# Attention and feed-forward on one core: four attention visits per tile, the first value copy on another queue, one mask tile

## The chip, the cores and the metric

The kernel runs on one core of one Trainium2 chip. The metric is device time in microseconds of one execution; lower is better. The kernel before took 334.62 us (median of 3 runs, 332.96 to 336.87). Its profiled execution has a span of 328.2 us, and all times inside the profile count from the start of that span.

The core has five engines that run side by side and wait for one another through semaphores. TensorE multiplies matrices (rows PE for matmuls and PEld for weight loads), VectorE (DVE) and ScalarE (ACT) work on elements, GpSimd (POOL) casts and copies here and issues transfers, and SyncE (SP) issues transfers. Matmul results go to PSUM banks; everything else lives in SBUF.

## What is computed

```python
# attention: batch 8, heads 8, sequence 576, head size 64; a query sees keys at most 32 away
scores = (1 / sqrt(64)) * q @ k.T
scores = where(abs(pos[:, None] - pos[None, :]) <= 32, scores, -1e9)
attn = exp(scores - max(scores));  attn = attn / (sum(attn) + 1e-9)
x = (attn @ v) laid out as (4608 tokens, 512)
# feed-forward: 512 -> 2048 -> 512
h = x @ w_in
g = 0.5 * h * (1 + tanh(sqrt(2/pi) * (h + 0.044715 * h**3)))
out = g @ w_out
```

## The kernel before

The 4608 tokens are nine FFN tiles of 512 (t = 0 to 8). While tile t is in its second FFN product, the attention of batch b = t + 1 is done in between. A plan says before which FFN-out matmul (0 to 111) which step comes: `s` scores and their exp, `m` mask, `v` weighted sum of values, `x` spread of the result into `xT`. The digit is the pair of heads (0 to 3); 4 is the batch's tail of queries for all pairs, and -1 is the tail of the batch before. A group of `s` and `v` at one place is called a visit below: TensorE leaves the FFN matmuls and comes back.

```python
PLAN = {5: "s0 v-1", 25: "m0 x-1", 27: "s1 v0", 40: "m1 x0", 49: "s2 v1", 62: "m2 x1",
        71: "s3 v2", 84: "m3 x2", 93: "s4 v3", 105: "m4", 112: "x3"}
PLAN_0 = {0: "w0 w1 m0", 10: "s-1 m-1", 16: "s1 v-1 w2 m1 x-1", 24: "s2 v0 w3 x0", 32: "m2 s3 v1 x1",
          40: "m3 v2 x2", 48: "t4", 51: "v3 c1 x3", 57: "s4 c2 m4"}      # tile 0

def score(b, g):
    m, prs, steps, slots, q0, n = work_of(b, g)
    ps = psS.tile([128, 2, 512], FP32, name="ps_s", tag=score_bank())    # S0 and S1 in turn
    ...                                                                  # 16 small matmuls: QT, KT -> ps
    nc.scalar.activation(pe, ps[:, :, 0:w], AF.Exp, scale=SCALE)

def mask(b, g, hs=slice(0, 2)):
    m, prs = work_of(b, g)[0:2]
    pe = groups[(b, g)][:, hs, :].rearrange("k h (r q) -> k (h r) q", r=len(prs))
    nc.vector.tensor_tensor(
        pe, pe, m.rearrange("k (o j) p -> k o (j p)", o=1).broadcast_to(list(pe.shape)), op=ALU.mult)

def weigh(b, g, other=False):
    ...
    o = bank(1) if other else psO.tile([128, 512], FP32, name="ps_o", tag="O")
    d = psO.tile([128, 512], FP32, name="ps_d", tag="D")
    ...                                   # d: 2 matmuls ones x pe; o: 14 (tail: 8) matmuls V x pe

def invert(b, g, o, d):                   # lt = exp(-ln(d)), two ScalarE instructions
def spread(b, g, o, lt):                  # xT = o * lt, on VectorE
```

There is one bank `O` and one bank `D`, and two pairs of score banks, `S0` and `S1`. The masks are four tiles, each built from pieces of a band `full`:

```python
kinds = [MAIN, TAIL, MAIN_0, TAIL_0]
masks = [const.tile([128, 4, n], FP16, name=f"mask{i}") for i, n in enumerate((120, 24, 128, 16))]
for i, q0 in ((2, 0), (3, 128), (0, 0), (1, 120)):
    for step in kinds[i]:
        for half, piece in enumerate(step):
            if piece is not None:
                ...
                nc.vector.tensor_copy(masks[i][r, :, p0 - q0:p1 - q0], full[r, :, pp0:pp0 + p1 - p0])
```

Queries and keys of batches 2 and on are loaded on SyncE's queue, cast by VectorE and transposed by transfers on SyncE's queue. Values are loaded, with a cast, on GpSimd's queue; then a copy inside SBUF puts each block also beside its neighbour on the other 64 partitions:

```python
def load_qk(b):                           # qr, four kr, qt, kt: seven transfers
    nc.sync.dma_start(...)
def load_v(b):                            # five transfers
    nc.gpsimd.dma_start(V[:, c, :, :], v[b, ...])
def pair_v(b, copy, hs=slice(0, H)):
    V = Vs[b % 2]
    copy(V[64:128, 4:8, hs, :], V[64:128, 0:4, hs, :])
    copy(V[0:64, 4:7, hs, :], V[0:64, 1:4, hs, :])

for t in range(NT):
    b = t + 1
    ...
        for fc in range(begun, NF):
            ffn_in(t, fc)
            if t == 1 and fc == 6:        # a gate: no load of batch 2's values before this gelu
                nc.gpsimd.tensor_copy(after, gTs[1][:, column(1, 5), 0:1])
                load_v(2)
                unpaired.append(2)
    if t and b + 1 < B:
        load_qk(b + 1)
    if t == 1:
        pair_v(unpaired.pop(), nc.sync.dma_start)
    ...                                   # the plan and the FFN-out matmuls; in v-1: load_v(b + 1)
    if unpaired:
        pair_v(unpaired.pop(), nc.sync.dma_start)
```

The first attention (batch 0) comes before any FFN work. It alternates transposes of the next pair (`turn`), their copies out (`trans_out`), masks, value pairing (`paired`) and `spin`, matmuls without use that keep TensorE busy:

```python
score(0, 0); spin(2, 512); pt = turn(1)
mask(0, 0)
trans_out(0, 1, pt)
spin(4, 512); score(0, 1); cast_vt(0); spin(2, 512); pt = turn(2)
paired(0)
mask(0, 1)
trans_out(0, 2, pt)
weighed(0); score(0, 2); spread(0, 0, *ods[0]); spin(5, 512)
paired(1); weighed(1); pt = turn(3)
trans_out(0, 3, pt)
mask(0, 2)
spin(3, 512, score=True); score(0, 3); spread(0, 1, *ods[1])
paired(2); weighed(2); mask(0, 3); ffn_in(0, 0, 0, 2); spread(0, 2, *ods[2])
paired(3); weighed(3)
```

Of the kernel before, what the change touches and what calls it, by code (L numbers as in the profile page):

```python
# [36 lines left out]
def cut(b):  # L37
# [5 lines left out]

PLAN = {5: "s0 v-1", 25: "m0 x-1", 27: "s1 v0", 40: "m1 x0", 49: "s2 v1", 62: "m2 x1",
        71: "s3 v2", 84: "m3 x2", 93: "s4 v3", 105: "m4", 112: "x3"}

TURN_0 = {10: 0, 12: 1, 14: 2, 15: 3}
PLAN_0 = {0: "w0 w1 m0", 10: "s-1 m-1", 16: "s1 v-1 w2 m1 x-1", 24: "s2 v0 w3 x0", 32: "m2 s3 v1 x1",
          40: "m3 v2 x2", 48: "t4", 51: "v3 c1 x3", 57: "s4 c2 m4"}

ORDER_0 = ([(t4, 4 * w + i) for w in range(4) for t4 in (0, 1)
            for i in ((2, 3, 0, 1) if w == 0 else range(4))] +
# [7 lines left out]
def kernel(  # L64
# [45 lines left out]
    full = const.tile([128, 4, 56], FP16, name="full")  # L110
    ones = const.tile([128, 64], FP16, name="ones")
    after = const.tile([128, 1], FP16, name="after")
    kinds = [MAIN, TAIL, MAIN_0, TAIL_0]
    masks = [const.tile([128, 4, n], FP16, name=f"mask{i}") for i, n in enumerate((120, 24, 128, 16))]
    KTs = [const.tile([128, NPAIR, 576], FP16, name=f"KT{i}") for i in range(2)]

    Vs = [const.tile([128, 8, H, 64], FP16, name=f"V{i}") for i in range(2)]
# [102 lines left out]
    def spin(n, width, score=False):  # L220
        ps = psS.tile([128, 2, 512], FP32, name="spin2", tag="S0")[:, 0, :] if score else \
            psO.tile([128, 512], FP32, name="spin", tag="O")
        for _ in range(n):
# [10 lines left out]
    nc.gpsimd.memset(idn, 0.0)  # L234
    nc.gpsimd.affine_select(out=idn, in_=idn, compare_op=ALU.not_equal, fill=1.0,
                            base=0, pattern=[[-1, 128]], channel_multiplier=1)
    for i, q0 in ((2, 0), (3, 128), (0, 0), (1, 120)):
        for step in kinds[i]:
            for half, piece in enumerate(step):
                if piece is not None:  # L240
                    k0, p0, p1 = piece
                    r, pp0 = slice(64 * half, 64 * half + 64), p0 - ((k0 - 64 * half) // 4 - 8)
                    nc.vector.tensor_copy(masks[i][r, :, p0 - q0:p1 - q0], full[r, :, pp0:pp0 + p1 - p0])  # L243
    nc.vector.memset(ones, 1.0)

    halfs = {}
# [50 lines left out]
    def bank(i):  # L297

        return psM.tile([128, 512], FP32, name="mm", tag=f"x{i}")
# [29 lines left out]


    groups = {}
    turns = [0]

    def score_bank():
        turns[0] ^= 1
        return f"S{turns[0] ^ 1}"


    def work_of(b, g):

        if g < 4:
            return (masks[0], [g], MAIN, SLOTS, 0, 120) if b else (masks[2], [g], MAIN_0, SLOTS_0, 0, 128)
        p0 = cut(b)
        return (masks[1 if b else 3], range(NPAIR), TAIL if b else TAIL_0, [(7, p0, 144)], p0, 144 - p0)

    def score(b, g):
        m, prs, steps, slots, q0, n = work_of(b, g)
        ps = psS.tile([128, 2, 512], FP32, name="ps_s", tag=score_bank())
        for r, pr in enumerate(prs):
            for step in steps:  # L350
                for half, piece in enumerate(step):
                    if piece is None:
                        continue
                    k0, p0, p1 = piece
                    for h in range(2):
                        r0 = 64 * h
                        nc.tensor.matmul(  # L357
                            ps[64 * half:64 * half + 64, h, 4 * n * r:4 * n * r + 4 * n].rearrange(
                                "k (j p) -> k j p", j=4)[:, :, p0 - q0:p1 - q0],
                            KTs[b % 2][r0:r0 + 64, pr, k0:k0 + 64],  # L360
                            QTs[b][r0:r0 + 64, pr, :, p0:p1], start=True, stop=True)
        w = 4 * n * len(prs)
        pe = ap_.tile([128, 2, w], FP16, name="pe", tag="pe") if g < 4 else \
            tailp.tile([128, 2, w], FP16, name="pet")
        nc.scalar.activation(pe, ps[:, :, 0:w], AF.Exp, scale=SCALE)  # L365
        groups[(b, g)] = pe

    def mask(b, g, hs=slice(0, 2)):
        m, prs = work_of(b, g)[0:2]
        pe = groups[(b, g)][:, hs, :].rearrange("k h (r q) -> k (h r) q", r=len(prs))  # L370
        nc.vector.tensor_tensor(  # L371
            pe, pe, m.rearrange("k (o j) p -> k o (j p)", o=1).broadcast_to(list(pe.shape)), op=ALU.mult)

    def weigh(b, g, other=False):
        m, prs, steps, slots, q0, n = work_of(b, g)
        pe = groups.pop((b, g))
        o = bank(1) if other else psO.tile([128, 512], FP32, name="ps_o", tag="O")
        d = psO.tile([128, 512], FP32, name="ps_d", tag="D")
        for h in range(2):
            nc.tensor.matmul(d[64 * h:64 * h + 64, 0:4 * n * len(prs)], ones, pe[:, h, :],  # L380
                             start=True, stop=True)
        for r, pr in enumerate(prs):
            cols = slice(4 * n * r, 4 * n * r + 4 * n)
            for i, (slot, p0, p1) in enumerate(slots):
                for h in range(2):
                    nc.tensor.matmul(  # L386
                        o[64 * h:64 * h + 64, cols].rearrange("d (j p) -> d j p", j=4)[:, :, p0 - q0:p1 - q0],
                        Vs[b % 2][:, slot, 2 * pr + h, :],
                        pe[:, h, cols].rearrange("k (j p) -> k j p", j=4)[:, :, p0 - q0:p1 - q0],
                        start=True, stop=True)  # L390
        return o, d
# [228 lines left out]
        pair_v(0, nc.vector.tensor_copy, slice(2 * g, 2 * g + 2))  # L620

    ods = {}
    score(0, 0)
    spin(2, 512)
    pt = turn(1)
    mask(0, 0)
    trans_out(0, 1, pt)
    spin(4, 512)
    score(0, 1)
    cast_vt(0)  # L630
    spin(2, 512)
    pt = turn(2)
    paired(0)
    mask(0, 1)
    trans_out(0, 2, pt)
    weighed(0)
    score(0, 2)
    spread(0, 0, *ods[0])
    spin(5, 512)
    paired(1)  # L640
    weighed(1)
    pt = turn(3)
    trans_out(0, 3, pt)
    mask(0, 2)
    spin(3, 512, score=True)
    score(0, 3)
    spread(0, 1, *ods[1])
    paired(2)
    weighed(2)
    mask(0, 3)  # L650
    ffn_in(0, 0, 0, 2)
    spread(0, 2, *ods[2])
    paired(3)
    weighed(3)
    for fc in (1, 2, 3):
        ffn_in(0, fc, 0, 2)
# [36 lines left out]
                       psO.tile([128, 8, 128], FP16, name="pt", tag="O"))  # L693
        ffn_in(0, fc)
    load_table(exp_set)
    score(1, 0)


    begun = 0
    for t in range(NT):  # L700
        b = t + 1
        att = b < B
        if t:
# [5 lines left out]
                cast_and_turn(b)  # L709
            for fc in range(begun, NF):  # L710
                ffn_in(t, fc)
                if t == 1 and fc == 6:

                    nc.gpsimd.tensor_copy(after, gTs[1][:, column(1, 5), 0:1])
                    load_v(2)
                    unpaired.append(2)
        plan = PLAN_0 if not t else PLAN if att else {5: "v-1", 31: "x-1"} if t == B - 1 else {}
# [6 lines left out]
        if t and b + 1 < B:  # L724
            load_qk(b + 1)
        if t == 1:
            pair_v(unpaired.pop(), nc.sync.dma_start)
        ods = {}
        for i in range(113 if t else 65):
            for act in plan.get(i, "").split():  # L730
                kind, g = act[0], int(act[1:])
                if kind == "w":
                    cast_w(wo[g], w_out16[:, 4 * g:4 * g + 4, :])
                    if g == 2:
# [7 lines left out]
                        cast_tails(1, nc.gpsimd)  # L742
                        load_qk(2)
                elif kind == "t":
                    pt = psS.tile([128, 2, 8, 128], FP16, name="pt", tag=score_bank())
                    trans_tails(1, pt[:, 0])
                elif kind == "c":
                    if g == 1:
                        combine_w()
                    combine(g)  # L750
                elif kind == "s":
                    score(*group(g))
                elif kind == "m":
                    mask(*group(g))
                elif kind == "v":
                    bb, gg = group(g)
                    o, d = weigh(bb, gg)
                    ods[g] = (o, invert(bb, gg, o, d))
                    if t and g < 0 and b + 1 < B:
                        load_v(b + 1)  # L760
# [49 lines left out]
```

The softmax here doesn't subtract the row's maximum and nothing guards it: scores larger than these inputs give would overflow.

## Time and profile before

| stretch of the span, us | what runs | length, us | TensorE busy, us | mean granted clock |
|---|---|---|---|---|
| 0 to 42 | first attention, FFN-in of tile 0 | 42.00 | 33.80 | 1.00 |
| 42 to 64.6 | FFN-out of tile 0 with batch 1 | 22.60 | 19.86 | 1.00 |
| 64.6 to 77.5 | FFN-in of tile 1 | 12.90 | 12.90 | 1.00 |
| 77.5 to 113.2 | FFN-out of tile 1 with batch 2 | 35.70 | 20.02 | 0.81 |
| 113.2 to 144.5 | tile 2 with batch 3 | 31.30 | 31.21 | 1.00 |
| 144.5 to 175.9 | tile 3 with batch 4 | 31.40 | 31.31 | 1.00 |

Tiles 4 to 6 look like tiles 2 and 3. A line of a timeline gives start, length, engine, source line (L), operation, what is written and read, tile shape and count, and in brackets how long the engine had been idle before and what ended that. SPq is SyncE's queue of transfers: its lengths are the time to issue, not the time to land. A line of the list of waits gives who waited for whom, then the total, the number of times and the longest. A line of stretches gives the stretch and its length, then the busy time of TensorE, its weight loads, VectorE, ScalarE and GpSimd, the mean granted clock of TensorE, the share of the DMA engines and GB/s.

### The profile page before, as it was taken

The page shows a single profiled execution, that of the slowest core. Times are in us where ns is not written, and L with a number is a line of the kernel's source. Part 1 is how long each engine was busy: PE and PEld are TensorE (multiplying, and loading weights), DVE is VectorE, ACT ScalarE, POOL GpSimd, SP SyncE. Part 2 cuts the span into 40 slices and gives each one's busy share as a digit, 9 for nine tenths or more (in the row PEclk, how much of TensorE's full clock was granted, in tenths as well). Part 3 has the DMA queues.
Part 4 walks back from the last instruction along what each step waited for, and adds up shares of the span by engine and source line. Part 5 has one row for each costly group of instructions (what it writes and reads, how often), then busy time and mean ns, then how long its engine had stood idle before and what let it go on. Part 6 is the DMA issues. An engine that isn't in the chain of part 4 may idle for free.

```text
span 328.2 us, 7176 instructions
## 1 busy us (share of the span) xinstructions
PE 295.6 (90%) x2883; PEld 183.5 (56%) x2883; DVE 195.0 (59%) x436; ACT 185.9 (57%) x283; POOL 106.6 (32%) x167
## 2 busy tenths in 40 slices
PE   5968996999109999999999999999999999999994
PEld 2434543446007746764685477547845874684483
DVE  6685477884206675586568655946585663443352
ACT  1366665467202677667856675677667766704700
POOL 3556368056000290048006600840080024007000
PEclk9999999999858999999999999999999999999999
DMA  7999999879990199959996999699875004004013
GB/s 212 253 368 359 385 259 240 202 140 143 223 204 17 33 186 196 222 129 148 215 210 151 167 233 187 133 170 248 147 158 110 10 11 120 0 2 128 2 32 96
DMA packets 117439, 52.90 MB, mean 161 GB/s; under 512 B 97935, under 2 KB 109967, under 8 KB 117406
## 3 DMA queue, kind: packets, MB, share of 16 engines
q1 hardware_dynamic: 84777, 40.12, 54.9%
q0 software_dynamic: 31696, 11.15, 31.6%
q10 hardware_dynamic: 933, 1.18, 1.2%
q8 instruction: 22, 0.36, 0.5%
q14 instruction: 11, 0.09, 0.1%
HBM read 36.70 MB, written 9.44 MB: 141 GB/s over the span
## 4 chain that ended last, share of the span: by engine, by line
PE 82%; DVE 5%; SPq 5%; ACT 2%; issue 2%; DMA 2%; POOL 0%; POOLq 0%
PE mm L542 30%; PE mm L447 20%; PE ph L447 16%; PE ps_s L357 4%; SPq L165 4%; PE mm L513 3%; PE ps_o L386 3%; PE ps_d L380 3%; DMA V<-V 2%; DVE mask L243 1%; DVE KT L293 1%; ACT pe L365 1%; PE pt L287 1%; PE spin L224 1%; PE pt L285 1%
## 5 line engine op out<-in xcount | busy, mean ns | idle before, releaser
L447 PEld LDWEIGHTS <-w_in 128*128 128x128 f16 x576 | 56.0, 98 | 66.1 <-issue 1.2
L503 POOL DMA_DIRECT2D out_dram<-y x77 | 46.6, 613 | 134.8 <-DVE y L571 134.2
L447 PE MATMUL mm<-xT,w_in 128*128 128x512 f16 x320 | 78.1, 379 | 0.0
L455 ACT ACTIVATE gT<-mm 128x512 f16<-128x512 f32 x80 | 47.6, 599 | 42.4 <-PE mm L447 41.8
L447 PE MATMUL ph<-xT,w_in 128*128 128x512 f16 x256 | 64.1, 379 | 0.7 <-ACT gT L455 0.7
L365 ACT ACTIVATE pe<-ps_s 128x960 f16<-128x960 f32 (+1 forms) x32 | 31.3, 977 | 56.1 <-PE ps_s L357 51.5
L487 DVE TENSOR_TENSOR s<-gT 128x512 f16<-128x512 f16 x64 | 26.9, 420 | 47.4 <-ACT gT L455 47.4
L542 PEld LDWEIGHTS <-s 128*128 128x128 f16 x512 | 48.8, 98 | 6.3
L542 PE MATMUL mm<-t,s 128*128 128x256 f16 x376 | 47.3, 275 | 0.0
L455 ACT ACTIVATE gT<-ph 128x512 f16<-128x512 f32 x64 | 36.3, 602 | 12.3 <-PE ph L447 12.1
L542 PEld LDWEIGHTS <-gT 128*128 128x128 f16 x384 | 36.9, 99 | 6.9
L542 PE MATMUL mm<-w_out,gT 128*128 128x256 f16 x256 | 32.4, 276 | 0.0
L386 PE MATMUL ps_o<-pe,V 128*64 128x64 f16 (+2 forms) x424 | 13.4, 200 | 18.2 <-DMA V<-V 14.6
L386 PEld LDWEIGHTS <-V 128*64 128x64 f16 x520 | 15.1, 112 | 25.1 <-DMA V<-V 14.7
L371 DVE TENSOR_TENSOR pe<-pe,mask 128x960 f16<-128x960 f16 (+1 forms) x32 | 23.5, 735 | 7.9 <-ACT pe L365 7.9
L399 ACT ACTIVATE lt<-ps_d 128x480 f32<-128x480 f32 (+3 forms) x40 | 22.0, 550 | 4.5 <-PE ps_o L386 3.5
L400 ACT ACTIVATE lt<-lt 128x480 f32<-128x480 f32 (+3 forms) x40 | 23.5, 587 | 1.3
L409 DVE TENSOR_TENSOR xT<-ps_o,lt 128x480 f16<-128x480 f32 (+5 forms) x38 | 20.2, 549 | 5.2 <-ACT lt L400 4.5
L89 ACT ACT_TABLE_LOAD x17 | 21.8, 1283 | 1.1 <-PEq L794 0.8
L173 POOL DMA_DIRECT2D V<-in_v_dram x24 | 21.5, 927 | 1.4 <-PE mm L447 1.4
L555 DVE TENSOR_TENSOR y<-mm,y 128x512 f32<-128x512 f32 x8 | 5.5, 692 | 24.7 <-PE mm L542 24.7
L357 PE MATMUL ps_s<-QT,KT 64*64 64x128 f16 (+3 forms) x648 | 16.1, 218 | 1.6 <-DVE KT L293 1.6
(79 smaller groups left out, 296.9 us busy)
## 6 DMA issues: line engine op xcount, KB each, us to landing
kr<-in_k_dram SPq DMA_DIRECT2D x32, 256.0 KB, 7.1
qr<-in_q_dram SPq DMA_DIRECT2D x6, 1024.0 KB, 10.9
wst<-in_moe_w_in_dram SPq DMA_DIRECT2D x3, 1024.0 KB
wst<-in_moe_w_out_dram SPq DMA_DIRECT2D x3, 1024.0 KB, 10.1
V<-in_v_dram POOLq DMA_DIRECT2D x24, 128.0 KB, 6.9
qr<-in_q_dram SPq DMA_DIRECT2D x8, 256.0 KB
vr<-in_v_dram SPq DMA_DIRECT2D x16, 128.0 KB, 5.5
V<-V SPq DMA_DIRECT2D x6, 256.0 KB
```

The source lines that it names most:

```text
L89: nc.scalar.add_instruction(mybir.InstLoadActFuncSet(name=nc.get_next_instruction_name(), act_func_set_id=which, ins=[], outs=[]))
L357: nc.tensor.matmul(ps[64 * half:64 * half + 64, h, 4 * n * r:4 * n * r + 4 * n].rearrange("k (j p) -> k j p", j=4)[:, :, p0 - q0:p1 - q0], ...
L365: nc.scalar.activation(pe, ps[:, :, 0:w], AF.Exp, scale=SCALE)
L371: nc.vector.tensor_tensor(pe, pe, m.rearrange("k (o j) p -> k o (j p)", o=1).broadcast_to(list(pe.shape)), op=ALU.mult)
L386: nc.tensor.matmul(o[64 * h:64 * h + 64, cols].rearrange("d (j p) -> d j p", j=4)[:, :, p0 - q0:p1 - q0], Vs[b % 2][:, slot, 2 * pr + h, : ...
L399: nc.scalar.activation(lt[:, 0:n], d[:, 0:n], AF.Ln)
L400: nc.scalar.activation(lt[:, 0:n], lt[:, 0:n], AF.Exp, scale=-1.0)
L447: nc.tensor.matmul(ph, w_in16[:, dc, fc * 128:fc * 128 + 128], xT[:, dc, t * 512 % RING:t * 512 % RING + 512], start=(dc == 0), stop=(dc = ...
L455: nc.scalar.activation(gTs[t][:, fc, :], phs[fc], AF.Gelu_apprx_tanh)
L487: nc.vector.tensor_tensor(dst, x, y, op=op)
L503: (eng or turn_about[0] if t == NT - 1 else eng or nc.gpsimd).dma_start(out_v[b, j, q0 + p:q0 + p + e, cols], yo[m:m + e, cols])
L542: nc.tensor.matmul(pys["apart"][:, 0:256] if apart else py[:, blk, :], lhsT, wino[w][:, f, :], start=(new and i % (8 if one else 16) == 0) ...
```

## The change

Attention gets four visits per tile in place of five. The first takes the scores of two pairs at once and the tail's products; the second one score and two products; the plan now says which score banks a step uses (`@0`, `@1`). For the second product of a visit, `O` and `D` are not free, so it goes into a pair of score banks. The four mask tiles become one, `band`, ordered by query, from which each use takes its columns; it is built in six copies. Batch 2's value copies go out on GpSimd's queue instead of SyncE's, and the gate before that load opens three gelus sooner. In the first attention, transposed keys are copied out ahead of the mask, and the pairing of values moves.

```diff
-PLAN = {5: "s0 v-1", 25: "m0 x-1", 27: "s1 v0", 40: "m1 x0", 49: "s2 v1", 62: "m2 x1",
-        71: "s3 v2", 84: "m3 x2", 93: "s4 v3", 105: "m4", 112: "x3"}
+PLAN = {4: "s0@0 s1@1 v-1", 26: "m0 x-1", 33: "m1", 34: "s2@0 v0 v1@1", 50: "m2 x0", 56: "x1",
+        62: "s3@0 v2", 82: "m3 x2", 91: "s4@1 v3", 105: "m4", 112: "x3"}
-PLAN_0 = {0: "w0 w1 m0", 10: "s-1 m-1", 16: "s1 v-1 w2 m1 x-1", 24: "s2 v0 w3 x0", 32: "m2 s3 v1 x1",
-          40: "m3 v2 x2", 48: "t4", 51: "v3 c1 x3", 57: "s4 c2 m4"}
+PLAN_0 = {0: "w0 w1 m0", 10: "s-1@0 s1@1", 15: "m-1", 16: "w2 m1", 20: "s2@1 v-1 v0@0", 24: "w3 x-1 x0 m2",
+          30: "s3@1 v1", 36: "m3 x1", 42: "v2 v3@0", 48: "t4 x2", 51: "x3 c1", 56: "s4@1", 57: "c2 m4"}
...
+    band = const.tile([128, 4, 144], FP16, name="band")
...
+    def blocks(r, p0, n, pp0, w):
+        nc.vector.tensor_copy(
+            band[r, :, p0:p0 + n * w].rearrange("k j (n p) -> k j n p", n=n),
+            full[r, :, pp0:pp0 + w].rearrange("k j (o p) -> k j o p", o=1).broadcast_to([64, 4, n, w]))
+    blocks(even, 0, 1, 8, 24)
+    blocks(odd, 0, 1, 8, 40)
+    blocks(even, 24, 3, 0, 32)
+    blocks(odd, 40, 2, 16, 32)
+    blocks(odd, 104, 1, 16, 40)
+    blocks(even, 120, 1, 0, 24)
...
-        pe = groups[(b, g)][:, hs, :].rearrange("k h (r q) -> k (h r) q", r=len(prs))
+        pe = groups[(b, g)][:, hs, :].rearrange("k h (r j p) -> k (h r) j p", r=len(prs), j=4)
         nc.vector.tensor_tensor(
-            pe, pe, m.rearrange("k (o j) p -> k o (j p)", o=1).broadcast_to(list(pe.shape)), op=ALU.mult)
+            pe, pe, m.rearrange("k (o j) p -> k o j p", o=1).broadcast_to(list(pe.shape)), op=ALU.mult)
...
-        o = bank(1) if other else psO.tile([128, 512], FP32, name="ps_o", tag="O")
-        d = psO.tile([128, 512], FP32, name="ps_d", tag="D")
+        if pair is not None:
+            od = psS.tile([128, 2, 512], FP32, name="ps_od", tag=f"S{pair}")
+            o, d = od[:, 0, :], od[:, 1, :]
+        else:
+            o = bank(1) if other else psO.tile([128, 512], FP32, name="ps_o", tag="O")
+            d = psO.tile([128, 512], FP32, name="ps_d", tag="D")
...
     pt = turn(1)
+    trans_out(0, 1, pt)
     mask(0, 0)
-    trans_out(0, 1, pt)
...
     pt = turn(2)
+    trans_out(0, 2, pt)
     paired(0)
     mask(0, 1)
-    trans_out(0, 2, pt)
     weighed(0)
...
     pt = turn(3)
+    paired(2)
     trans_out(0, 3, pt)
...
-    paired(2)
     weighed(2)
     mask(0, 3)
+    paired(3)
     ffn_in(0, 0, 0, 2)
     spread(0, 2, *ods[2])
-    paired(3)
     weighed(3)
...
-                if t == 1 and fc == 6:
-                    nc.gpsimd.tensor_copy(after, gTs[1][:, column(1, 5), 0:1])
+                if t == 1 and fc == 3:
+                    nc.gpsimd.tensor_copy(after, gTs[1][:, column(1, 2), 0:1])
                     load_v(2)
...
         if t == 1:
-            pair_v(unpaired.pop(), nc.sync.dma_start)
+            pair_v(unpaired.pop(), nc.gpsimd.dma_start)
```

## The prediction

> **What bounds the kernel now.** I read the page first (busy shares and slices), then the list of waits, then the stretches of time cut at the tile boundaries, then the timelines around whatever stood out.
>
> The page says TensorE is the bound, apart from one hole:
>
> ```profile
> PE 295.6 (90%) x2883; PEld 183.5 (56%) x2883; DVE 195.0 (59%) x436; ACT 185.9 (57%) x283; POOL 106.6 (32%) x167
> ...
> PE   5968996999109999999999999999999999999994
> ...
> PEclk9999999999858999999999999999999999999999
> ```
>
> A slice is 8.2 us. Slices 11 and 12 (82 to 98 us) are nearly empty of matmuls, and the granted clock falls to 0.8 and 0.5 after them. The list of waits names the hole (total, times, longest):
>
> ```profile
> PE ps_o L386 <- DMA V<-V: 14.6, 1, 14.6
> ```
>
> It is batch 2's value copy, SBUF to SBUF, wanted by the first product of scores and values. Cut by stretches, the FFN-out half of tile 1 takes 35.70 us with 20.02 us of matmul at a mean clock of 0.81; a whole steady tile takes 31.40 us with TensorE busy throughout:
>
> ```profile
> 77.50:113.20 35.70, 20.02 (x272) 15.12 (x271) 13.53 (x26) 13.28 (x19) 2.47 (x5) 0.81 1.02 120
> ...
> 144.50:175.90 31.40, 31.31 (x332) 20.27 (x330) 20.90 (x49) 21.74 (x34) 11.43 (x17) 1.00 1.24 181
> ```
>
> Why the copy is late stands on the SyncE queue's timeline (start, length):
>
> ```profile
> 78.17 12.32 SPq L165 DMA_DIRECT2D kr<-in_k_dram  x4
> 90.53 0.95 SPq L167 DMA_DIRECT2D qt<-in_q_dram  x1
> 91.53 0.66 SPq L168 DMA_DIRECT2D kt<-in_k_dram  x1
> 92.43 0.53 SPq L180 DMA_DIRECT2D V<-V  x1
> 93.01 0.59 SPq L181 DMA_DIRECT2D V<-V  x1
> ```
>
> and on GpSimd's, which loads the values:
>
> ```profile
> 70.52 0.38 POOL L714 COPY after<-gT 128x1 f16<-128x1 f16 x1 [4.03 <-ACT gT L455]
> 70.84 3.57 POOL L173 DMA_DIRECT2D V<-in_v_dram  x4
> ```
>
> The copy is issued at 92.43 us, behind batch 3's key loads in program order, though the values themselves had landed by 79.9 (the fourth of these loads went out at 73.5 and took 6.4 us).
>
> **What the skill says.** "DMA: Bandwidth & Descriptors", section "Queues, rings and completion order": each DMA engine takes turns, packet by packet, between the queues that have work. So a copy in GpSimd's queue need not wait for all of the key loads ahead of it in SyncE's. The trace agrees that the old place costs: 12.32 us of issuing stands ahead of the copy. The same page, "Issuing engines are not separate DMA queues", warns that all queues share the same engines: only the wait to be issued goes away, not the traffic. "TensorEngine Tiling (Array Packing)", section "Tiling Modes": a change of tiling mode drains TensorE. The trace agrees in direction; I size it below. "VectorE: DVE Perf Modes", section "What auto-detection actually checks": the two-per-cycle mode of a two-input operation asks for 16-bit data with step one. The new mask operand is four runs of 120 instead of one of 480, still step one. The old mask takes 0.65 us for 960 elements, which at the page's 0.96 GHz is more than one per cycle; I take no change.
>
> **Part 1, batch 2's copies to GpSimd's queue.** The gate before the load moves from the sixth gelu of tile 1 to the third. The third gelu ends near 68.4 us (three of them fill 67.33 to 68.90), so the load starts about 2.1 us earlier and lands at 79.9 - 2.1 = 77.8. GpSimd then issues the two copies in about 1.3 us. On SyncE the second took 5.8 us from issue to landing at the tail of the key loads; I allow 3 to 6 us, so landing at 82 to 85, in the old clock. It is wanted by v0, at matmul 34 instead of 27. From 78.29, 34 matmuls take 3.7 us (one is 0.109 us: sixteen go from 163.95 to 165.70), visit A 1.2, the scores of visit B 0.4: 83.6. So a wait of 0 to 1.5 us is left of 14.6. Tile 1 ran from 64.6 to 113.2, 48.6 us, against 31.3 for a steady tile: 17.3 lost, of which the wait is 14.6 and the rest the slow clock after it and a 0.95 us mask wait. Tile 1 also has two 1.22 us weight combinations on VectorE ahead of the masks, so I leave it 2.7 us over a steady tile: **-14.6 us**.
>
> **Part 2, four visits instead of five (six tiles).** This is visit 2 and visit 3 of a steady tile on TensorE:
>
> ```profile
> 162.47 0.39 PE L380 MATMUL ps_d<-pe,ones 128*64 128x480 f16 x2
> 162.96 0.50 PE L386 MATMUL ps_o<-pe,V 128*64 128x96 f16 x14
> 163.39 0.72 PE L542 MATMUL mm<-t,s 128*128 128x256 f16 x5
> ...
> 165.70 0.27 PE L542 MATMUL mm<-t,s 128*128 128x256 f16 x1
> 165.90 0.40 PE L357 MATMUL ps_s<-QT,KT 64*64 64x96 f16 x16
> 166.23 0.39 PE L380 MATMUL ps_d<-pe,ones 128*64 128x480 f16 x2
> 166.46 0.40 PE L386 MATMUL ps_o<-pe,V 128*64 128x96 f16 x14
> 166.79 2.58 PE L542 MATMUL mm<-t,s 128*128 128x256 f16 x22
> ```
>
> Visit 3: the next FFN matmul would start at 165.81 and starts at 166.79, 0.98 us. Parts: entry 0.09, scores 0.33, sums 0.23, products with the way out 0.33. In visit 2 the products start 0.49 after the sums instead of 0.23: they wait for the product bank, held until VectorE has spread the tail. Taken the same way the five visits cost 0.88, 1.35, 0.98, 1.00, 1.02: 5.23 us. The four new ones: A (two scores, tail products) 0.09+0.33+0.33+0.18+0.27 = 1.20; B (one score, two products) 0.09+0.33+2x0.56 = 1.54; C and D 1.00 each: 4.74. So 0.49 us less, if nothing new waits.
>
> Something does: v1 needs mask 1. ScalarE's table load ends at 160.31, then exp 0 and exp 1 (0.87 apart), then ln and exp of the tail's sums (0.52 apart): the tail's inverse is ready near 163.1. VectorE runs in order: mask 0, the tail's spread (to 163.7), the output add of matmul 31 (0.61), mask 1 (0.65): 164.9. TensorE gets to v1 at 164.2. That is 0.7 us of new waiting, so 0.49 - 0.7 = +0.2 per tile. Tile 1's wait is already in part 1; five tiles: **+1 us**.
>
> **Part 3, one mask tile, and the first attention reordered.**
>
> ```profile
> 2.04 4.55 DVE L243 COPY mask<-full 64x96 f16<-64x96 f16 x21 [0.84 <-POOL full L232]
> 4.13 0.61 POOL L256 CAST k<-kr 128x512 f16<-128x512 f32 x1 [1.61 <-DMA kr<-in_k_dram]
> 6.79 0.43 DVE L256 CAST q<-qr 128x512 f16<-128x512 f32 x1
> ```
>
> VectorE builds masks until 6.6 us while the first keys are there at 4.13, so the first transpose waits for masks, and the chain of waits passes through them. 21 copies at 217 ns become 6, with half the elements: 1.3 us by count, 2.3 by elements, so done near 3.8. The query cast can start at 4.1, and TensorE, whose warm-up ends at 4.86, at 4.9 instead of 7.28: 2.4 us. Key transposes going out ahead of the masks take 0.95 and 0.47 us of TensorE waits (at 17.27 and 21.28). Not all survives: DMA casts pace this stage, and in tile 0 v0 moves from matmul 24 to 20 while its values are paired by GpSimd only at 48.0. I carry **-2.8 us** to the end of tile 0.
>
> Sum: -14.6 + 1 - 2.8 = -16.4; 334.6 - 16.4 = 318.2, say **318 us**.
>
> **Rivals.** (a) *The copy is still late*: at 80 to 84 us loads already fill the DMA engines, and batch 3's value loads took up to 11.6 us from issue to landing there. If the copy takes as long, it lands near 90: 5 or 6 us of wait return, and the clock falls again: 324 to 326. Against it: the copy is few, long pieces, and now stands ahead of batch 3's value loads. (b) *The merged visits cost more than they save*: s1 needs the second pair's keys 3.3 us earlier, whose transpose is issued only near 151.3; if it lands after 159.1, each tile waits 1 to 2 us: 324 to 330. No landing of these transposes is shown; a small one issued at 156.51 took 5.9, which puts this one near 158. (c) *The new order runs clean*, with no wait for mask 1: 0.5 us gained in each of five tiles, and 4 us at the start: 313. (d) *The start is held by DMA*: loads already move 333 to 391 GB/s from 16 to 44 us, so work starting sooner may only wait sooner: 321.
>
> **Range and chances.** The 2% line is 6.7 us away from 334.6, and part 1 alone is more than twice that; to miss it takes (b) at its worst, or (a) together with a start that gains nothing and some of (b). Range 311 to 326. Faster by over 2% (under 327.9): 0.93; within 2%: 0.05; slower: 0.02.
>
> **What would show it.** Right: no wait of TensorE for the V copy over 2 us and a clock of 1.0 through tile 1; steady tiles of 31 to 31.7 us with 4 visits, and a wait of the sums (ps_od) for the mask in the second; first transpose near 4.9 us. Wrong: a long wait for V<-V; a wait of ps_s for a DMA into KT; steady tiles over 32.5 us or masks well over 0.65 us; the first FFN matmul still near 23.5 us.

## The result and the profile after

The changed kernel takes 320.21 us (median of 4 runs, 319.21 to 321.12) where the kernel before, run beside it, takes 334.22 (332.96 to 336.87): a ratio of 0.957, 95% interval 0.950 to 0.964. The prediction was 318.0 within 311 to 326.

The two traces have spans of 328.2 and 317.5 us, so they show 10.7 of the 14.0 us between the medians (the execution of before that was profiled was quicker than its timed ones). Cut at the first FFN-in matmul of each tile:

| stretch | before, us | after, us | difference |
|---|---|---|---|
| start to tile 1 | 64.48 | 62.16 | -2.3 |
| tile 1 | 48.60 | 37.58 | -11.0 |
| tiles 2 to 6, sum | 156.59 | 159.63 | +3.0 |
| tiles 7, 8 and end | 58.5 | 58.1 | -0.4 |

The hole in the slices of the page is narrower (a slice is 7.9 us now). It lies in slice 11, from 79 to 87 us, and the granted clock falls in it and in the next. So it did before: the prediction put the fall of the clock after slices 11 and 12, but its own line has the 8 and the 5 in these two slices.

```profile
PE   6779997999499998999999999999999999999994
...
PEclk9989999999789999999999999999999999999998
```

Two rows of the list of waits, TensorE's two longest (total, times, longest), give the rest of the story. The wait for batch 2's value copy (the parts of `V` that one transfer copies to another place in `V`) fell from 14.6 us to 4.0, and a wait that the kernel before did not have came in, five times:

```profile
PE ps_o L388 <- DMA V<-V: 4.0, 1, 4.0
PE ps_od L382 <- DVE pe L369: 2.8, 5, 0.9
```

In stretches, the FFN-out half of tile 1 and one steady tile (length, then busy time of TensorE, its loads, VectorE, ScalarE and GpSimd, then the clock):

```profile
75.97:99.74 23.77, 19.22 (x267) 15.05 (x266) 13.32 (x26) 12.79 (x18) 5.90 (x9) 0.86 1.29 181
...
163.85:195.73 31.88, 31.16 (x333) 20.32 (x330) 20.90 (x52) 21.61 (x34) 11.31 (x16) 1.00 1.09 178
```

The work of that half is the same 19 to 20 us of matmul. The idle time in it fell from 15.7 us to 4.6, and the clock there rose from 0.81 to 0.86. The steady tile lost half a microsecond (31.40 to 31.88).

The timeline of all engines in tile 1 shows where the 4.0 us come from. The values have landed by 77.37, GpSimd issues the two copies at once, they land 7.8 and 8.3 us after their issue, and TensorE goes on at 86.30:

```profile
76.77 0.40 SPq L162 DMA_DIRECT2D qr<-in_q_dram  x1
...
77.37 0.55 POOL L179 DMA_DIRECT2D V<-V  x1 [5.96 <-DMA V<-in_v_dram]
77.91 0.55 POOL L180 DMA_DIRECT2D V<-V  x1
...
86.30 0.53 PE L388 MATMUL ps_o<-pe,V 128*64 128x64 f16 x12 [4.04 <-DMA V<-V]
```

Note the first line: 0.6 us ahead of the copies, SyncE sends out batch 3's query load, 1 MB in one transfer. The experiments come back to it.

The timeline of TensorE in tile 4, second visit, shows the new wait, and VectorE's in the same stretch shows its cause. First TensorE:

```profile
184.35 0.39 PE L382 MATMUL ps_od<-pe,ones 128*64 128x480 f16 x2 [0.56 <-DVE pe L369]
```

VectorE runs in order. It spreads the tail's product, adds the output of the FFN (L557), and only then masks the second pair (L369), for which TensorE waits:

```profile
182.57 0.56 DVE L417 TENSOR_TENSOR xT<-ps_o,lt 128x384 f16<-128x384 f32 x1 [0.60 <-ACT lt L402]
183.05 0.68 DVE L557 TENSOR_TENSOR y<-mm,y 128x512 f32<-128x512 f32 x1
183.65 0.65 DVE L369 TENSOR_TENSOR pe<-pe,band 128x960 f16<-128x960 f16 x1
```

At the start, the timeline shows the six band copies done at 3.4 us, the query cast behind them waiting only for its load, and the first transpose at 4.65 instead of 7.28:

```profile
2.04 1.34 DVE L237 COPY band<-full 64x96 f16<-64x96 f16 x6 [0.84 <-POOL full L231]
3.64 0.43 DVE L260 CAST q<-qr 128x512 f16<-128x512 f32 x1 [0.19 <-DMA qr<-in_q_dram]
4.65 0.58 PE L289 MATMUL pt<-idn,q 128*128 128x128 f16 x4
```

Steady FFN-in of tile 0 then begins at 24.09 (25.97 before), and tile 1 at 62.16 (64.48).

### The profile page after: what moved, and what is told of

It reads as the page before. It is cut to its first block, busy times and chain, and to the rows that moved or that the text cites. A ratio compares the mean times of both kernels' runs of the same rounds, so it can differ in the third digit from the quotient of the medians.

```text
span 317.5 us, 7161 instructions
## 1 busy us (share of the span) xinstructions
PE 294.2 (93%) x2883; PEld 184.0 (58%) x2883; DVE 191.2 (60%) x421; ACT 185.1 (58%) x283; POOL 109.2 (34%) x169
## 4 chain that ended last, share of the span: by engine, by line
PE 61%; DMA 17%; DVE 8%; ACT 5%; SPq 5%; POOL 2%; issue 1%; DVEq 0%; POOLq 0%
PE mm L544 24%; PE mm L449 16%; PE ph L449 13%; DMA wst<-in_moe_w_in_dram 3%; DMA vr<-in_v_dram 3%; DMA KT<-k 3%; DMA V<-V 3%; DMA qr<-in_q_dram 2%; DVE pe L369 2%; PE mm L515 2%; DMA V<-in_v_dram 2%; ACT pe L363 2%; PE ps_o L388 2%; SPq L133 2%; SPq L142 2%
## 5 line engine op out<-in xcount | busy, mean ns | idle before, releaser
L544 PEld LDWEIGHTS <-s 128*128 128x128 f16 x512 | 49.6, 98 | 6.0
L363 ACT ACTIVATE pe<-ps_s 128x960 f16<-128x960 f32 (+1 forms) x32 | 30.6, 976 | 37.7 <-PE ps_s L355 20.8
L544 PE MATMUL mm<-t,s 128*128 128x256 f16 x376 | 44.7, 273 | 0.0
L544 PE MATMUL mm<-w_out,gT 128*128 128x256 f16 x256 | 34.2, 281 | 0.0
L369 DVE TENSOR_TENSOR pe<-pe,band 128x960 f16<-128x960 f16 (+1 forms) x32 | 21.7, 679 | 1.0 <-ACT pe L363 1.0
L401 ACT ACTIVATE lt<-ps_d 128x480 f32<-128x480 f32 (+3 forms) x32 | 17.5, 548 | 4.2 <-PE ps_d L382 3.8
L559 DVE COPY y<-mm 128x512 f32<-128x512 f32 x8 | 5.5, 691 | 20.3 <-PE mm L544 20.3
L515 PE MATMUL mm<-w_out,gT 128*128 128x512 f16 x64 | 15.6, 380 | 1.5 <-DVE yo L519 1.2
L544 PE MATMUL mm<-t,gT 128*128 128x256 f16 x128 | 16.3, 273 | 0.0
L355 PE MATMUL ps_s<-QT,KT 64*64 64x128 f16 (+3 forms) x648 | 14.9, 215 | 1.5 <-DVE KT L297 0.7
```

What stands on the lines that cost most here:

```text
L369: nc.vector.tensor_tensor(pe, pe, m.rearrange("k (o j) p -> k o j p", o=1).broadcast_to(list(pe.shape)), op=ALU.mult)
L515: nc.tensor.matmul(pys[t4], gTs[0][:, fc, t4 * 128:t4 * 128 + 128], w_out16[:, fc, :], start=new, stop=(fc == NF - 1))
L544: nc.tensor.matmul(pys["apart"][:, 0:256] if apart else py[:, blk, :], lhsT, wino[w][:, f, :], start=(new and i % (8 if one else 16) == 0) ...
```

## The experiments

Ratios are to the kernel before, run on the same chip in the same batch; its medians there were 334.16 (1 to 3), 335.8 (4 to 7), 332.64 (8 to 10) and 334.07 us (11). Each ratio leaves out executions over 1.5% slower than the quickest of their kernel, which leaves two of four in the first kernel of 1 and one in 2, too few for a ratio there. Tile lengths are from each run's trace; these repeat to about 0.1 us in undisturbed tiles and are the sharper measure for one tile.

**1. The new copy alone, and the rest without it.** The first kernel is before plus part 1:

```diff
-                if t == 1 and fc == 6:
-                    nc.gpsimd.tensor_copy(after, gTs[1][:, column(1, 5), 0:1])
+                if t == 1 and fc == 3:
+                    nc.gpsimd.tensor_copy(after, gTs[1][:, column(1, 2), 0:1])
...
-            pair_v(unpaired.pop(), nc.sync.dma_start)
+            pair_v(unpaired.pop(), nc.gpsimd.dma_start)
```

> The kernel before with part 1 alone: batch 2's value copies on GpSimd's queue and the gate at the third gelu. My theory: nearly all of the gain is here, because tile 1 went from 48.6 to 37.6 us in the profiles, 11.0 us: 334.2 - 11 = 323, and a wait for the V copy of 3 to 5 us stays. Rival, that the start and the visits carry half of it: 327 or more. Rival, that the four visits cost time and the rest gains without them: under 321.

Measured: 322.33 us (318.82 to 325.79), ratio 0.9575 (0.949 to 0.966). Tile 1 takes 38.43 us with a wait for V of 4.2; the tiles after it take 31.30 to 31.37. This trace, of an execution of 325.14 us, begins tile 1 only at 70.21, where the kernel before, with the same start, began it at 64.48; what makes the start vary was not tried.

The second is the changed kernel with these lines turned back.

> The changed kernel with part 1 undone: copies back on SyncE's queue, gate at the sixth gelu. My theory: the long wait for the V copy returns (11 to 15 us), so about 320.2 + 11 = 331, that is within 1% of the kernel before, since the start gains 2.3 us and six tiles lose about 0.6 us each. Rival, that the visits and the start help: 328 or less.

Measured: 331.67 us, ratio 0.998 (0.995 to 1.001). Tile 1 takes 49.81 us with a wait for V of 16.0. Part 1 is therefore nearly the whole gain: alone it brings as large a ratio as the entire change (on two executions), and without it nothing is left that can be told from zero. The earlier start doesn't help here either: tile 1 begins at 62.09, then waits longer for the same copy, which goes out behind the key loads at 91.52.

**2. The old visits.** The changed kernel with five visits; score banks written out, products in `O` and `D` as before:

```diff
-PLAN = {4: "s0@0 s1@1 v-1", 26: "m0 x-1", 33: "m1", 34: "s2@0 v0 v1@1", 50: "m2 x0", 56: "x1",
-        62: "s3@0 v2", 82: "m3 x2", 91: "s4@1 v3", 105: "m4", 112: "x3"}
+PLAN = {5: "s0@0 v-1", 25: "m0 x-1", 27: "s1@1 v0", 40: "m1 x0", 49: "s2@0 v1", 62: "m2 x1",
+        71: "s3@1 v2", 84: "m3 x2", 93: "s4@0 v3", 105: "m4", 112: "x3"}
```

> The changed kernel with the five visits of before in tiles 1 to 6 (tile 0 and all else as changed). My theory: the four visits cost 0.5 to 0.8 us per steady tile, through the wait of the second product for its mask, so steady tiles return from 31.8-32.1 to 31.3 us and the whole gains 3 to 4 us: about 317. Rival, that the longer tiles come from the mask's new form or from DMA: no change, 320, with tiles still near 31.9.

Measured: 318.5 us (313.04 to 320.18). The trace is clear: tiles 2 to 6 take 31.30 to 31.37 us, against 31.82 to 32.12 with the four visits, and tile 1 takes 40.09 with a wait for V of 6.0. Most of that longer wait comes from the values, which landed 1.75 us later (copies issued at 79.12 instead of 77.37); v0 asked only 0.3 us sooner (81.97 instead of 82.26). So the four visits as planned cost time in steady tiles; what they do in tile 1 this run does not show.

**3. The old start.** The changed kernel with the four mask tiles (21 copies) and the old order of the first attention, as the removed lines of the diff have them:

```diff
-    band = const.tile([128, 4, 144], FP16, name="band")
+    kinds = [MAIN, TAIL, MAIN_0, TAIL_0]
+    masks = [const.tile([128, 4, n], FP16, name=f"mask{i}") for i, n in enumerate((120, 24, 128, 16))]
...
```

> The changed kernel with part 3 undone: four mask tiles from 21 copies, and the first attention in the order of before. My theory: FFN-in of tile 1 starts at 64.5 instead of 62.2 us, and the time is 2 to 3 us longer: 322.5 to 323. Rival, that the start is held by DMA and the 2.3 us came from the plan of tile 0: 320 to 321. It also shows whether the mask's form matters in the steady tiles: mean of a 128x960 mask 0.65 us in both if not.

Measured: 323.74 us (322.7 to 328.04), ratio 0.970 (0.963 to 0.977). The first transpose falls back to 7.30 us and tile 1 begins at 63.50 instead of 62.16: 1.3 us. Later two waits for transposed keys (4.1 us in total) appear, in tiles 1 and 3; tile 3 takes 33.48. How the start brings those about was not tried. The form of the mask makes no difference: from 131 to 260 us a mask of 128x960 takes 0.65 us on average with either, and undisturbed tiles take 31.82 us with either.

**4. Mask 1 ahead of the output sum.** One number of the plan: VectorE gets the second mask before matmul 31's output add.

```diff
-PLAN = {4: "s0@0 s1@1 v-1", 26: "m0 x-1", 33: "m1", 34: "s2@0 v0 v1@1", 50: "m2 x0", 56: "x1",
+PLAN = {4: "s0@0 s1@1 v-1", 26: "m0 x-1", 30: "m1", 34: "s2@0 v0 v1@1", 50: "m2 x0", 56: "x1",
```

> The changed kernel with mask 1 three places sooner in the plan (30 instead of 33), so that VectorE does it ahead of the output add of matmul 31. My theory: the second product waits 0.6 us per tile for mask 1 because that add stands ahead of it in VectorE's order; then the wait falls to about 0.1 us or nothing, steady tiles go from 31.82 to 31.2-31.3 us, and the time from 320.2 to about 317. Rival, that the wait comes from ScalarE (table load, two exps, ln): mask 1 starts no sooner, tiles stay within 0.1 us of 31.82.

Measured: 316.8 us (316.39 to 317.1), ratio 0.950 (0.943 to 0.958). On VectorE's timeline the order is turned:

```profile
181.64 0.56 DVE L417 TENSOR_TENSOR xT<-ps_o,lt 128x384 f16<-128x384 f32 x1 [0.60 <-ACT lt L402]
182.12 0.65 DVE L369 TENSOR_TENSOR pe<-pe,band 128x960 f16<-128x960 f16 x1
182.68 0.68 DVE L557 TENSOR_TENSOR y<-mm,y 128x512 f32<-128x512 f32 x1
```

and on TensorE's the sums of the second pair follow with no idle time:

```profile
182.35 0.50 PE L388 MATMUL ps_o<-pe,V 128*64 128x96 f16 x14
182.82 0.39 PE L382 MATMUL ps_od<-pe,ones 128*64 128x480 f16 x2
```

Steady tiles take 31.22 us (one of 31.89, with a wait of 0.9 for a transposed key), 0.6 less than with the mask behind the add. So that wait was the whole cost of the four visits. But they now beat the five old ones (31.31) by only 0.09.

**5. The key loads later.** To see whether batch 3's loads hold up the copies, `load_qk(3)` was moved behind matmul 36 of tile 1:

```diff
-        if t and b + 1 < B:
+        if t > 1 and b + 1 < B:
             load_qk(b + 1)
...
+            if t == 1 and i == 36:
+                load_qk(b + 1)
```

> The changed kernel with batch 3's query and key loads held back in tile 1 until matmul 36, behind the first value products. Theory that the V copy takes 8.3 us because it shares the DMA engines with these loads: it lands 3 to 4 us after its issue, the wait of 4.0 us goes, tile 1 falls from 37.6 to about 33 us and the time to 316. Rival, that the copy is slow by itself, or is held by the stores and value loads of its own queue: the wait stays at 3 to 6 us, time 320 or worse since the keys come late for tile 2.

Measured: 320.79 us (319.55 to 321.28), ratio 0.961 (0.951 to 0.972); wait for V 3.7. Whether the loads hold up the copies, this run does not answer. The edit moved the load in the program, but nothing on SyncE stands between the two places: its queue ran ahead and sent the query load at 77.72, before the copies (78.79), just as in the kernel after.

**6. The copies by GpSimd itself.**

```diff
-            pair_v(unpaired.pop(), nc.gpsimd.dma_start)
+            bv = unpaired.pop()
+            for pr in range(NPAIR):
+                pair_v(bv, nc.gpsimd.tensor_copy, slice(2 * pr, 2 * pr + 2))
```

> The changed kernel with batch 2's value copies done by GpSimd itself, pair of heads by pair, instead of by a transfer. In tile 0 GpSimd takes about 1.3 us for one pair. Values land at 77.3 us, so pair 0 is there near 78.7 and pair 1 near 80, before TensorE asks at 81.5 and 82.5. Theory: no wait for V is left, tile 1 falls from 37.6 to about 33 us, time 316. Rival, that copies on GpSimd stretch VectorE's masks and adds (one mask took 2.63 us in tile 0 of the kernel before while GpSimd copied): a mask wait of 1 to 2 us takes the place, 318.

Measured: 319.03 us (316.53 to 320.97), ratio 0.957 (0.944 to 0.969); tile 1 37.56. The wait for V<-V is gone, but the values landed only at 80.34, and waits for transposed keys of 3.7 us took its place.

**7. The loads as early as can be.** `load_v(2)` goes out at the end of tile 0, without the gate:

```diff
-                if t == 1 and fc == 3:
-                    nc.gpsimd.tensor_copy(after, gTs[1][:, column(1, 2), 0:1])
-                    load_v(2)
-                    unpaired.append(2)
...
         if t == 0:
+            load_v(2)
+            unpaired.append(2)
             load_table(gelu_set)
...
-        if unpaired:
+        if t and unpaired:
```

> The changed kernel with batch 2's value loads issued at the end of tile 0, with no gate in tile 1 (the copies stay on GpSimd's queue at their place). Theory: values land at least 3 us sooner, near 72-74 us, and the copies go out before batch 3's key loads start at 77, so the wait of 4.0 us shrinks to 0-1 us: about 316 to 317. Rival, that the loads then collide with the end of batch 2's key loads and the transposes: s0 of tile 1 waits for a transpose, time 319 to 321.

Measured: 315.96 us (315.27 to 320.71), ratio 0.947 (0.938 to 0.957). The profiled execution, at 320.71 us, lost 6 us in tile 2 (37.83), to two waits for transposed keys (1.72 and 1.80) and a clock of 0.5 from 113 to 120 us. Its tile 1 takes 32.84 us with no wait for V. The loads went out only 0.75 us sooner than in the kernel after (65.75 against 66.50), and the values landed no sooner (77.46), but this time the copies landed 4.9 and 5.2 us after their issue. The timeline of all engines shows what is different:

```profile
77.46 0.55 POOL L179 DMA_DIRECT2D V<-V  x1 [6.71 <-DMA V<-in_v_dram]
78.00 0.55 POOL L180 DMA_DIRECT2D V<-V  x1
78.08 1.11 SPq L162 DMA_DIRECT2D qr<-in_q_dram  x1
```

Here the copies went out 0.6 us ahead of the query load. What each queue moved, in MB per microsecond, shows who was served first (the copies are 0.46 MB on GpSimd's queue, the query load 1 MB on SyncE's):

| from, us | 79 | 80 | 81 | 82 | 83 | 84 |
|---|---|---|---|---|---|---|
| after: SyncE's queue | 0.17 | 0.35 | 0.34 | 0.29 | 0.02 | 0.03 |
| after: GpSimd's queue | 0 | 0 | 0 | 0.07 | 0.21 | 0.19 |
| loads early: SyncE's queue | 0.11 | 0 | 0.05 | 0.26 | 0.34 | 0.33 |
| loads early: GpSimd's queue | 0.13 | 0.22 | 0.11 | 0 | 0 | 0 |

In both, the transfer that was issued first moved first, and the other began as it ended. Two readings stood after this. Theory A: VectorE's dense run at 79 to 84 us keeps GpSimd from writing the copies' descriptors (the orders to the DMA engines). The Trainium skill describes such a block ("SBUF — State Buffer", section "SBUF: two separate sides", on the "DVE blocks DMA" trap) for operations of VectorE in a two-port mode, and says that ScalarE's and SyncE's queues don't have it. All but one of the operations in that run are two-input ones (TENSOR_TENSOR), and no trace shows their mode. Theory B: the copies stand behind what was issued before them.

**8. The copies on ScalarE's queue.**

```diff
-            pair_v(unpaired.pop(), nc.gpsimd.dma_start)
+            pair_v(unpaired.pop(), nc.scalar.dma_start)
```

> Batch 2's two value copies are issued by ScalarE's queue instead of GpSimd's; nothing else changes. In the traces so far the copies' first packets move 4.7 to 5.1 us after their issue on GpSimd where VectorE is in its dense run (after: issued 77.37, first packets after 82.5), and 2.0 us after it where VectorE is idle in between (the kernel with the earliest loads: 77.46, 79.5). Theory A (the descriptors that GpSimd writes are held up by VectorE's run): from ScalarE's queue no descriptors are written by GpSimd, so the copies land within 4 us of their issue, TensorE's wait for V falls from 4.0 us to under 0.8, tile 1 takes 32.5 to 34.5 us instead of 37.6, and the time is 315 to 317.5. Theory B (the copies stand behind other transfers in the DMA engines): they land 7 to 8 us after issue as before, tile 1 stays at 37 to 38, the time at 320. Theory C (ScalarE, in order, is held by the wait for the loads): the exponentials of visit A come late instead, the wait moves from V to the score banks, and the time is 318 to 321.

Measured: 322.36 us (321.28 to 323.54), ratio 0.970 (0.962 to 0.978); tile 1 takes 40.45 us. The copies went out at 78.20 and 79.22, and TensorE got V at 88.73:

```profile
71.78 3.53 POOL L172 DMA_DIRECT2D V<-in_v_dram  x4
77.46 0.40 SPq L162 DMA_DIRECT2D qr<-in_q_dram  x1
78.20 0.51 ACTq L179 DMA_DIRECT2D V<-V  x1
...
88.73 0.53 PE L388 MATMUL ps_o<-pe,V 128*64 128x64 f16 x12 [4.20 <-DMA V<-V]
```

By the skill's account under 7, GpSimd writes no descriptor of these copies, and TensorE gets V 9.5 us after the second all the same. So theory A is not needed for a late copy. It is not ruled out as a part of the delay on GpSimd's queue, because this kernel differs in one more thing. The first line shows a side effect that I had not seen coming: GpSimd, which no longer waits to issue the copies, sends batch 3's value loads at 71.78, ahead of them instead of behind. Theory B's numbers (7 to 8 us, tile 1 at 37 to 38) were exceeded too, and theory C came in part: ScalarE, busy with issuing, starts the exponentials of visit A at 80.74 (78.08 in the kernel after), and TensorE waits 2.1 us (0.42, 0.84 and 0.85) before it even asks for V.

This trace also shows how queues share the engines. From 86 to 87 us the copies move on ScalarE's queue (q10) beside SyncE's (q1) and GpSimd's (q0); a line gives packets, MB, and the share of the engines:

```profile
q10 hardware_dynamic: 67, 0.16, 68.6%
q1 hardware_dynamic: 65, 0.07, 29.7%
q0 software_dynamic: 66, 0.01, 12.9%
```

The packet counts are nearly equal, so three queues with work took turns packet by packet. In the table under 7 there are no turns: from 80 to 82 us the kernel after moved 673 packets of SyncE's queue and none of GpSimd's. From the two together I infer that the copies' packets were not yet there for the engines to take. What held them before that point, no run shows.

**9. VectorE's weight differences earlier.** The copies stay on GpSimd's queue; VectorE's dense run is broken up.

```diff
-        if t == 1 and i > 2 and i in wino["todo"]:
-            combine(i)
...
+                if t == 1 and fc in (8, 9):
+                    combine({8: 17, 9: 33}[fc])
```

> The copies stay on GpSimd's queue; VectorE's two weight differences of tile 1 (1.22 us each, at 79.63 and 82.97 in the trace of after) are made earlier, in the FFN-in of tile 1, where VectorE waits 1.9 us per step. The same work, only VectorE's run behind the copies' issue is broken up. Theory A (VectorE holds up GpSimd's descriptors): the first packets move 1 to 3 us sooner after the issue than 5.1, the wait for V falls from 4.0 to 1 to 3 us, tile 1 takes 34.5 to 36.7, the time is 317 to 319.5. Theory B (transfers of other queues are ahead): first packets still about 5 us after the issue, wait 4.0, tile 1 at 37 to 38, time 320.

Measured: 321.25 us (320.16 to 321.72), ratio 0.966 (0.959 to 0.974); the copies landed 9.6 and 9.8 us after issue, the wait for V is 6.4, tile 1 takes 39.78. The query load was again ahead (76.64 against 77.57) and filled the engines from 79 to 83; the copies' first packets moved after 82, about 5 us after issue, as theory B had it. Theory A's gain did not come, but the test is weak: VectorE was still busy for 2.5 of the 3 us from 79 to 82. Theory B's wait of 4.0 and its 37 to 38 us for tile 1 failed too; why the copies landed later than in the kernel after stays open.

**10. Mask first, with the copies on ScalarE's queue.** The edits of 4 and 8 together.

> Two changes to after: mask 1 ahead of the output sum on VectorE in every tile (alone: steady tiles 31.22 instead of 31.85, time 316.8) and batch 2's value copies on ScalarE's queue. If the two losses are separate, they add: steady tiles 31.2 to 31.3, tile 1 at 32 to 34, the time 311.5 to 314. If ScalarE's wait for the loads takes the place of the wait for V, tile 1 stays at 36 to 37 and the time at 315.5 to 317.

Measured: 320.05 us (319.35 to 321.2), ratio 0.962 (0.953 to 0.971). Steady tiles 31.22 to 31.29 (one 31.92), tile 1 42.07: the gain of the mask is there, and the loss of the queue is larger. As in 8, batch 3's value loads went out first (71.14; the copies at 77.49 and 80.62), and the exponentials of visit A started late (81.14).

**11. Mask first, with the copies ahead of the query load.** SyncE takes the copies, and only then batch 3's loads:

```diff
+        if t == 1:
+            pair_v(unpaired.pop(), nc.sync.dma_start)
         if t and b + 1 < B:
             load_qk(b + 1)
-        if t == 1:
-            pair_v(unpaired.pop(), nc.gpsimd.dma_start)
```

> After with two edits: mask 1 ahead of the output sum (alone 316.8, tile 1 37.15 us, steady tiles 31.22), and batch 2's value copies put on SyncE's queue ahead of batch 3's query and key loads, where before they stood behind them. Why: in all traces with late copies the 1 MB query load of batch 3 was issued 0.3 to 2.4 us before the last copy, and it moved first (after: 1.15 MB on SyncE's queue from 79 to 83, the copies' 0.47 MB after that); in the one trace with copies that landed in 5 us the copies were issued 0.6 us before the query load, and their packets came first. Theory B (the DMA engines serve in order of issue, and the copies stood behind the query load): the copies are issued at 77.5 to 78.5 when the values land, their first packets follow within 2.5 us, they land by 82.5 to 84, TensorE's wait for V is 0 to 1.2 us instead of 4.2, tile 1 takes 32 to 34, and the time is 311.5 to 314. Theory D (a copy of 64 partitions to the other 64 takes 7 to 8 us in this phase whatever is ahead): wait 4, tile 1 37, time 316 to 317.5. Rival E: SyncE, held until the values land, issues batch 3's loads later, and tile 2 loses what tile 1 gains: tile 2 over 33 us, time 315 to 317.

Measured: 318.81 us (316.78 to 319.74), ratio 0.957 (0.951 to 0.963). Steady tiles 31.22 to 31.28 (one 32.02), but tile 1 takes 40.19, with a wait for V of 5.7. The copies did go out ahead of the query load. The timeline shows what was ahead of them instead:

```profile
71.19 3.53 POOL L172 DMA_DIRECT2D V<-in_v_dram  x4
...
77.14 0.55 SPq L179 DMA_DIRECT2D V<-V  x1
77.74 1.65 SPq L180 DMA_DIRECT2D V<-V  x1
79.44 0.59 SPq L162 DMA_DIRECT2D qr<-in_q_dram  x1
```

From 80 to 82 us GpSimd's queue moved batch 3's values, some 850 packets and 0.11 MB per microsecond, and the copies' bytes came mostly from 82 to 86. Rival E did not show (tile 2 takes 31.22). My 32 to 34 us for tile 1 was wrong, for the side effect of 8, which I should have carried over to this kernel.

What this leaves: in eleven kernels (after and ten others) a queue sent the copies as the values landed. In ten of them the query load or batch 3's values had been issued first, and the copies took 7.4 us or more; in the one where neither had, they took 5. That speaks for theory B in this form: what was issued before makes the copies late, though not by keeping the engines from taking turns. It rests on that one trace for the positive side: a kernel that deliberately puts the copies ahead of both (on GpSimd's queue, with the query load held behind them) was not run. So the delay by earlier transfers is likely, and not shown; theory D is spoken against by that one trace alone. The versions that beat the changed kernel's 0.957 are 4 (0.950) and 7 (0.947), one number and one moved load; their intervals overlap with its own, and for 4 the steady tiles in the trace (31.22 for 31.82) confirm the gain.

## Why the prediction was right, point by point

**Part 1 (-14.6): right in kind, 3.6 us too good.** Measured -11.0 in tile 1. The gate was as expected: the load went out 4.3 us sooner (70.84 to 66.50), 2.3 of them because tile 1 began sooner. That the values landed at 77.37 where 77.8 was predicted is luck: the 77.8 stood in the old clock, and 2.3 us sooner makes 75.5, so they were 1.9 late. The term that failed most is "I allow 3 to 6 us" for the copies' landing: it was 7.8 and 8.3. I had taken it from a copy at the end of the key loads. I had also argued from the Trainium skill ("DMA: Bandwidth & Descriptors", section "Queues, rings and completion order") that a copy on its own queue takes turns with the loads. Such turns are there in the trace of 8 (67, 65 and 66 packets), but they did not help: for over 3 us, from 79 to 82.5, the engines moved only the query load, though the copies had been issued 0.6 us after it. The step that failed is to take a queue of its own for a place in these turns. The wait became 4.0 instead of 0 to 1.5. During it the clock fell to 0.5, as it did during the long wait of before, and it stayed low for about 4 us after: from 87.57 to 92.08, 28 FFN matmuls took 4.5 us where a steady tile has 3.2 for them. The predicted 2.7 us over a steady tile became 6.3, and 4.0 + 1.3 of these are the wait and the clock. This is rival (a), with 4.0 us of wait where it named 5 or 6.

**Part 2 (+1): right in mechanism, +3.0 measured.** The sums of the second product wait for mask 1, because VectorE adds the output first: predicted 0.7 us, measured 0.24 to 0.86, and experiment 4 removes it by turning the two round. The term that failed is the 0.49 us saved by a visit fewer: with the wait gone, 0.09 is saved. Measured as the prediction did it, in the trace of experiment 4, the four visits cost 1.09 + 1.82 + 0.98 + 1.30 = 5.19 us, not 4.74. A came out cheaper (1.20 predicted), but the second product wait of the old visit 2 did not go away: B's first products start 0.38 after the sums and take 0.47, and D's start 0.55 after them, held by VectorE's spread (xT). I had counted each at 0.23 and 0.33. Rival (b), late keys of the second pair, came once (0.56 us in tile 3).

**Part 3 (-2.8): near in size, shown for about half.** The first transpose moved to 4.65 (predicted 4.9), and 2.3 us reached the end of tile 0. Experiment 3 gives 1.3 us of that back; the other 1.0 is, by difference, not from the masks or the order of the first attention, and the new plan of tile 0 was not tried alone. These are single traces, and the old start gave 64.48 in one and 70.21 in another. That rival (d) also holds in part is seen in two other traces (the copy turned back in 1, and 8), where FFN-in of tile 0 first begins at 19.5 to 20.2 instead of 21.2 and tile 1 still not before 62.1. In the first of them TensorE then waits in tile 0 for casts of queries (0.77 us) and weights (0.30 and 0.37) and for the pairing of values by GpSimd (0.94).

**The sum.** The steps make -14.6 + 1 - 2.8 = -16.4; the traces show -11.0 + 3.0 - 2.3 - 0.4 = -10.7 and the medians -14.0. The misses of parts 1 and 2, 3.6 and 2.0 us, go the same way. The time came out closer than the steps (2.2 us above the prediction), and that is luck: the profiled execution of before, on which the steps stand, was some 4 us quicker than its median, and the steps were taken off the median. What the slower ones spend that time on, no trace of that kernel shows. By the signs that the prediction itself named, its "no wait for V over 2 us", its clock of 1.0 through tile 1 and its "steady tiles of 31 to 31.7" (31.82 to 32.12) failed; the wait for the mask in the second visit and the first transpose near 4.9 held.

## What to carry to other kernels

In these traces a late transfer was late where something large had been issued just before it, on whatever queue. Before moving a transfer to another queue, list what goes out in the few microseconds ahead of it, and what the queue's owner will send sooner once it no longer waits. When two pieces of work on an in-order engine feed different consumers, put the one that the bound engine asks for first; here one number of a plan was worth 0.6 us per tile. Moving a load in the program moves nothing if its engine has nothing in between to wait for.

## What the runs showed of the hardware

While a 1 MB load of 1 KB packets moved (79 to 82.5 us, up to 0.35 MB per microsecond), a 0.46 MB copy that had been issued 0.6 us after it on another queue did not move at all; with the order of issue turned round by 0.6 us, the copy moved first. Where packets of several queues were under way together, the engines took them in turns: 67, 65 and 66 packets of three queues in one microsecond.

The value loads with a cast to 16 bits move in packets of about 130 bytes, and at 0.11 MB per microsecond where they moved almost alone (80 to 82 us in 11). A batch's values are some 0.6 MB in 16 bits, so at this rate they take 5 us, against 3 us for 1 MB of queries at 0.34: an estimate from these rates.

In the trace of after, TensorE waits from 82.26 to 86.30. The granted clock falls to 0.50 between 83 and 84, within the wait, and is back at 1.00 by 91, some 4 us after it. With the 1.3 us that the 28 matmuls lost, this wait cost at least a third more than its length.
